# Retention attention before a sine feed-forward: bursts in four 64x64 tiles, head-wise loads of two batches, and decay and state hand-on on GpSimd

## Chip, cores and metric

One core of one Trainium2 chip. The metric is device time of one execution in microseconds (us), from several executions of each kernel. Kernels that are compared ran in the same rounds on one chip; experiments 1 to 4 ran on one chip and 5 to 12 on another, where the kernel before took 219.49 and 219.7 to 219.8 us. "The profile" is one execution recorded by the hardware profiler; "the trace" is its list of instructions. PE is TensorE, PEld its weight loads, DVE VectorE, ACT ScalarE, POOL GpSimd, SP SyncE. In the code, matmuls write tiles of PSUM; all other tiles stand in SBUF. All times and ratios of the text are of fast runs; one run of the kernel before (222.21 us, slow) is left out of the ratios.

## The reference, cut to what matters

```python
# q, k, v: 4 batches x 8 heads x 768 positions x 64, float32
for t in range(S):                                   # attention: a decaying state per head
    state = gamma[h] * state + outer(k[t], v[t])
    y[t]  = scale * (q[t] @ state)
x = y as [3072 tokens, 512]
h = x @ w_in                                         # 512 -> 2048
g = h + sin(alpha * h) ** 2 / (alpha + 1e-9)
out = g @ w_out                                      # 2048 -> 512
```

Both kernels cut the 768 positions into six chunks of 128. For a chunk after the first of its batch, the work on TensorE is a **burst**: *inter* (state times q), *scores* (k times q, then masked), *mix* (v times masked scores) and *sums* (k times v, the addition to the state). Bursts are put between the dense matmuls of the feed-forward, which runs over seven groups of chunks; group g+1's chunks are made while group g is in the feed-forward. The order is: the four first chunks (group 0), then batch 0's other five, batch 1's, batch 2's, batch 3's. Chunks are numbered in that order from 0: 4 is the first after the four first chunks, and 14 is the first of batch 2 after its first chunk, and 14 to 23 are batches 2 and 3. One group's feed-forward is a *phase*, cut into 16 *slots* (8 in the groups of two chunks), and a burst or a part of it is put into a slot. In the code cuts `P[n]` is chunk n and `e1` to `e3` are the first chunks of batches 1 to 3; the numbers before the brackets are slots, with T a transpose on TensorE, X one by DMA, A the scores, M inter and mix, SK the sums of a first state, and B a whole burst.

## The kernel before, where the change touches it

```python
def load_chunk(j, names="qkv"):            # 128 positions x 8 heads: 1024 rows a DMA
    ...
            nc.gpsimd.dma_start(out=t, in_=chunk_of(src, j))
def turn(j):                               # q, k transposed by a DMA of SyncE's queue
    nc.sync.dma_start_transpose(out=st["qkT", j], in_=raw["qk", j]...)
def stage_A(j):                            # scores: two tiles of 64 rows at a time
    ...
    nc.tensor.matmul(pa[:, e, p, :], qkT[r, NP + p, :], qkT[r, p, :], ...)
    nc.vector.tensor_mul(aT, pa, mask)
def stage_S(j):                            # sums: the state accumulates in PSUM
    nc.tensor.matmul(ps[64*e:64*e+64, p, :], raw["k", j][...], raw["v", j][...], start=(c == 0 and p == 0), ...)
def keep_S(j, ps):                         # hand-on: ScalarE casts it for the next chunk
    for e in range(2):
        nc.scalar.copy(s_bd[(j % NCH + 1) % 2][r, :, r], ps[r, :, :])
# ... (cut: transposes, stage_M with inter and mix, the Slot class of the feed-forward)
# GpSimd's order: each later chunk's three loads, with one earlier chunk's decay of v between
for n in range(11, NJ + 2):
    scale_v(P[n - 2], nc.gpsimd)
    if n < NJ:
        load_chunk(P[n])
    if n in (13, 15):
        scale_v(P[(n - 9) // 2], nc.gpsimd)
```

## Time and profile before

| | before |
|---|---|
| time, median of 3 runs | 219.66 us (219.4 to 219.67) |
| profiled span | 217.5 us |
| TensorE busy | 94 % of the span |
| decays of v on GpSimd | 21 of 1.056 us |
| q, k, v loads by GpSimd | 70 of about 0.9 us each |

The page's slices divide the span into 40 equal parts; a digit is the busy share in tenths, and PEclk is TensorE's granted clock in tenths of full speed. Before:

```profile
POOL 8975335999889885896981000000000000000000
PEclk9999999999999999999999999999999999999999
```

GpSimd is a queue of loads with decays between them, at work until slice 21 (about 117 us; with gaps in slices 3 to 6) and idle after. The lines that carry the reading of TensorE stand in the prediction below.

### The profile page before, as it was taken

What the parts mean: (1) busy time and instruction counts of PE and PEld (TensorE: products, weight loads), DVE (VectorE), ACT (ScalarE), POOL (GpSimd) and SP (SyncE); (2) the same over time, 40 slices, a digit from 0 to 9 for tenths busy, and PEclk for the clock granted to TensorE, in tenths of its full rate; (3) what the DMA queues carried; (4) which work ended last, traced back from release to release, by engine and by line L of the source; (5) the groups of instructions that cost most, each with busy time, mean ns of one, the idle gap of its engine ahead of it and who ended that gap; (6) DMA issues with size and microseconds to landing.
All of it is one profiled execution on the core that took longest, in us unless ns stands there. A gap on an engine that the chain in (4) does not pass through costs nothing.

```text
span 217.5 us, 4218 instructions
## 1 busy us (share of the span) xinstructions
PE 203.8 (94%) x1634; PEld 107.5 (49%) x1661; DVE 128.1 (59%) x213; ACT 162.8 (75%) x311; POOL 90.1 (41%) x105
## 2 busy tenths in 40 slices
PE   7798899999989999999999999999999999999992
PEld 3444554467764545445455445454544544555540
DVE  4686659867895767766466566366464555233310
ACT  7678796658889999789768768777868876766610
POOL 8975335999889885896981000000000000000000
PEclk9999999999999999999999999999999999999999
DMA  9999999999999999999999146237011101111121
GB/s 132 151 193 191 205 207 164 154 207 161 164 151 182 163 120 154 112 160 175 135 188 107 23 96 77 60 60 96 7 47 51 48 0 51 48 48 48 51 94 50
DMA packets 99508, 24.67 MB, mean 113 GB/s; under 512 B 92304, under 2 KB 96416, under 8 KB 99488
## 3 DMA queue, kind: packets, MB, share of 16 engines
q0 software_dynamic: 77024, 13.37, 84.0%
q1 hardware_dynamic: 22464, 11.02, 26.4%
q8 instruction: 13, 0.21, 0.4%
q14 instruction: 7, 0.06, 0.1%
HBM read 27.27 MB, written 6.29 MB: 154 GB/s over the span
## 4 chain that ended last, share of the span: by engine, by line
PE 74%; DVE 9%; DMA 4%; POOL 4%; ACT 4%; issue 3%; POOLq 0%; ACTq 0%
PE po L304 35%; PE ph L279 31%; DMA qkr<-in_k_dram 4%; DVE gT L294 4%; PE py L247 3%; PE pa L213 2%; POOL qkr L83 2%; ACT s L282 2%; DVE aT L217 2%; PE py L251 2%; POOL vr L83 1%; DVE xT L258 1%; PE ps L227 1%; DVE s L289 1%; ACT s L287 1%
## 5 line engine op out<-in xcount | busy, mean ns | idle before, releaser
L294 DVE SCALAR_TENSOR_TENSOR gT<-s,rec_alpha,ph 128x512 bf16<-128x512 f32 (+3 forms) x120 | 74.1, 637 | 68.1 <-ACT s L287 67.5
L279 PE MATMUL ph<-xT,w_in 128*128 128x512 bf16 (+3 forms) x478 | 97.9, 336 | 1.1 <-DVE gT L294 0.6
L304 PE MATMUL po<-w_out,gT 128*128 128x512 bf16 x360 | 94.1, 379 | 3.8 <-issue 2.9
L282 ACT ACTIVATE s<-ph,alpha_sb 128x512 f32<-128x512 f32 (+3 forms) x120 | 69.6, 601 | 34.0 <-PE ph L279 33.9
L279 PEld LDWEIGHTS <-w_in 128*128 128x128 bf16 x480 | 45.5, 98 | 42.6 <-issue 2.1
L287 ACT ACTIVATE s<-s 128x512 f32<-128x512 f32 (+1 forms) x94 | 58.4, 621 | 2.6
L304 PEld LDWEIGHTS <-gT 128*128 128x128 bf16 x384 | 35.2, 98 | 38.2 <-issue 0.6
L112 POOL TENSOR_TENSOR vr<-vr,kg 128x512 bf16<-128x512 bf16 x21 | 22.0, 1056 | 12.2 <-DMA vr<-in_v_dram 12.2
L217 DVE TENSOR_TENSOR aT<-pa,mask 128x1024 bf16<-128x1024 f32 x20 | 24.4, 1220 | 0.3 <-PE pa L213 0.3
L83 POOL DMA_DIRECT2D vr<-in_v_dram x24 | 21.7, 904 | 3.0 <-DMA w_in<-in_moe_w_in_dram 1.7
L83 POOL DMA_DIRECT2D qkr<-in_q_dram x23 | 21.3, 925 | 4.0 <-DMA w_out<-in_moe_w_out_dram 1.6
L83 POOL DMA_DIRECT2D qkr<-in_k_dram x23 | 20.4, 887 | 3.8 <-DMA w_out<-in_moe_w_out_dram 3.3
L234 ACT CAST s_bd<-ps 64x256 bf16<-64x256 f32 x40 | 14.4, 360 | 2.4 <-PE ps L227 2.1
L316 ACT COPY o_sb<-po 128x512 f32<-128x512 f32 x23 | 13.1, 576 | 3.9 <-PE po L304 3.9
L258 DVE TENSOR_TENSOR xT<-py,qg 128x512 bf16<-128x512 f32 x20 | 13.7, 684 | 2.6 <-PE py L251 2.5
L328 PE MATMUL spare<-warm 128*128 128x512 bf16 x27 | 9.3, 465 | 1.4 <-DVE warm L131 1.2
L213 PEld LDWEIGHTS <-qkT 64*128 64x128 bf16 x192 | 5.4, 94 | 9.3 <-issue 7.1
L251 PE MATMUL py<-aT,vr 128*64 128x128 bf16 x192 | 9.5, 220 | 0.4 <-DVE rec_alpha L366 0.2
L213 PE MATMUL pa<-qkT 64*128 64x128 bf16 x192 | 9.5, 219 | 0.4 <-ACT qkT L186 0.2
L247 PE MATMUL py<-qkT,s_bd 128*64 128x128 bf16 x160 | 8.3, 224 | 0.7 <-DVE xT L258 0.7
L247 PEld LDWEIGHTS <-s_bd 128*64 128x64 bf16 x160 | 5.4, 109 | 4.8 <-issue 2.0
L251 PEld LDWEIGHTS <-vr 128*64 128x64 bf16 x192 | 6.9, 110 | 1.3 <-issue 1.0
(59 smaller groups left out, 68.8 us busy)
## 6 DMA issues: line engine op xcount, KB each, us to landing
out_dram<-o_sb SPq DMA_DIRECT2D x24, 256.0 KB, 2.3
vr<-in_v_dram POOLq DMA_DIRECT2D x24, 128.0 KB, 6.2
qkr<-in_q_dram POOLq DMA_DIRECT2D x23, 128.0 KB, 5.6
qkr<-in_k_dram POOLq DMA_DIRECT2D x23, 128.0 KB, 5.8
w_in<-in_moe_w_in_dram POOLq DMA_DIRECT2D x4, 512.0 KB, 11.1
w_out<-in_moe_w_out_dram POOLq DMA_DIRECT2D x4, 512.0 KB, 14.8
q<-in_q_dram SPq DMA_DIRECT2D x1, 256.0 KB, 3.4
k<-in_k_dram SPq DMA_DIRECT2D x1, 256.0 KB, 4.7
```

Of the source, the lines that this page charges most:

```text
L83: nc.gpsimd.dma_start(out=t, in_=chunk_of(src, j))
L112: eng.tensor_mul(raw["v", j], raw["v", j], kg[:, j % NCH, :, None].to_broadcast([128, H, D]))
L213: nc.tensor.matmul(pa[:, e, p, :], qkT[r, NP + p, :], qkT[r, p, :], start=(p == 0), stop=True, skip_group_check=True)
L217: nc.vector.tensor_mul(aT.rearrange("p e n t -> p (e n) t"), pa.rearrange("p e n t -> p (e n) t"), m)
L247: nc.tensor.matmul(py[r, p, :], s_bd[c % 2][:, p, r], qkT[:, p, :], start=(p == 0), stop=True, skip_group_check=True)
L251: nc.tensor.matmul(py[64 * e:64 * e + 64, p, :], vs[:, 2 * p + e, :], aT[:, e, p, :], start=(c == 0 and p == 0), stop=True, skip_group_che ...
L258: nc.vector.tensor_mul(x, py, qg[:, c])
L279: nc.tensor.matmul(self.ph[:, m, :], w_in[:, i, f * 128:(f + 1) * 128], xT[g][:, i, self.lo:self.hi], start=(m == 0 and i == 0), stop=(i = ...
L282: nc.scalar.activation(out=self.s[:, m, :], in_=self.ph[:, m, :], func=ACTF.Sin, scale=alpha_sb[:, f:f + 1])
L287: nc.scalar.activation(out=self.s, in_=self.s, func=ACTF.Square)
L294: nc.vector.scalar_tensor_tensor(gT[self.g][:, f, self.lo:self.hi], self.s[:, m, :], rec_alpha[:, f:f + 1], self.ph[:, m, :], op0=ALU.mult ...
L304: nc.tensor.matmul(po[g, ts], gT[g][:, f, ts * C:(ts + 1) * C], w_out[:, f, :], start=(f == 0), stop=(f == FF - 1))
```

## The change

Its intent: shorter bursts (all four 64x64 tiles of TensorE at once; for batches 2 and 3 a head-wise layout that leaves out the scores above the diagonal and runs inter in the full array), VectorE's and ScalarE's burst work taken out of the way of the feed-forward's additions, and state and decay of the head-wise chunks on GpSimd, which has time late in the kernel. The diff cut to its core (cut: tables, masks, renamed tiles, the new start, the slot arithmetic):

```diff
+    def wide(j):                                   # the head-wise chunks
+        return j % NCH > 0 and j // NCH >= 2
+    def load_seq(bt):                              # a whole batch: 24 DMAs of 640 rows
+        for i, src in enumerate((q, k, v)):
+            for h in range(H):
+                nc.gpsimd.dma_start(out=o, in_=src[bt, h, C:, :].rearrange("(f i) d -> i f d", i=64))
     def load_w_in(i):                              # 1 DMA becomes 3; the last two exchange row halves
+        nc.gpsimd.dma_start(out=w_in[:, 0:2, c], in_=w_in_v[:, 0:2, c])
+        for y in range(2):
+            nc.gpsimd.dma_start(out=w_in[64 * y:64 * y + 64, 2:4, c], ...)
-    def keep_S(j, ps):                             # ScalarE, from PSUM
+    def keep(j, py, base=256):                     # VectorE adds the sums to a float state in SBUF
+            nc.vector.tensor_add(s_f, s_f, new)
+    def hand_on(j):
+        if not wide(j + 1):
+            nc.scalar.copy(s_n[i], s_f)
+            return
+        nc.gpsimd.tensor_copy(s[half(0), :, 0:4:3], s_f[half(0)])
+        nc.gpsimd.tensor_copy(s[half(1), :, 1:3], s_f[half(1)])
-    for n in range(11, NJ + 2):                    # loads and decays in turn
-        scale_v(P[n - 2], nc.gpsimd)
-        if n < NJ:
-            load_chunk(P[n])
+    load_chunk(P[11])
+    scale_v(P[9], nc.gpsimd)
+    load_chunk(P[12])
+    load_chunk(P[13])
+    load_seq(2)
+    load_seq(3)                                    # later decays and hand-ons stand behind these
-     5: [A(P[8]), M(P[7])], 6: [X(P[11]), A(P[9]), M(P[8]), SK(e1)], 7: [M(P[9])]}, 2)
+     5: [X(P[11]), B(P[8], P[9], e1)], 7: [B(P[9], P[10])]}, 2, calm=False, hold=6)
+    def burst(old, new, first=None):               # inter(old), scores(new), mix(old), sums
-    for fn in out_pieces(NG - 1, range(sizes[-1])):
+    for fn in out_pieces(NG - 1, range(sizes[-1] - 1)):
+    last_tile(NG - 1, sizes[-1] - 1)               # leaves in 256, 128 and 128 columns
```

## The prediction

> **What bounds the kernel now.** I read the page's totals first, then its chain of work that ended last, then TensorE's waits in the steady part, then the timeline of one attention burst, then GpSimd's timeline and the tail.
>
> ```profile
> PE 203.8 (94%) x1634; PEld 107.5 (49%) x1661; DVE 128.1 (59%) x213; ACT 162.8 (75%) x311; POOL 90.1 (41%) x105
> PE 74%; DVE 9%; DMA 4%; POOL 4%; ACT 4%; issue 3%; POOLq 0%; ACTq 0%
> ```
>
> TensorE is busy for 94% of the span and carries 74% of the chain. TensorE's own waits between 66 and 214 us are these, all of them:
>
> ```profile
> PE po L304 <- issue: 1.9, 12, 0.2
> PE py L247 <- DVE xT L258: 0.2, 1, 0.2
> PE ph L279 <- ACT o_sb L316: 0.2, 1, 0.2
> ```
>
> So for 148 us no other engine is in TensorE's way: only less TensorE work helps there, and every new wait costs its full length. (Waits just under the view's cut add some 0.6 us around 78 and 88 us.) One burst in that part, in TensorE's timeline with its weight loads:
>
> ```profile
> 100.26 1.03 PE L279 MATMUL ph<-xT,w_in 128*128 128x512 bf16 x4
> ...
> 101.22 0.40 PE L213 MATMUL pa<-qkT 64*128 64x128 bf16 x8
> ...
> 101.55 0.41 PE L247 MATMUL py<-qkT,s_bd 128*64 128x128 bf16 x8
> ...
> 101.79 0.39 PE L251 MATMUL py<-aT,vr 128*64 128x128 bf16 x8
> ...
> 102.02 0.29 PE L227 MATMUL ps<-vr,qkr 128*64 128x64 bf16 x8
> 102.23 0.55 PEld L304 LDWEIGHTS <-gT 128*128 128x128 bf16 x4
> 102.47 0.81 PE L304 MATMUL po<-w_out,gT 128*128 128x512 bf16 x3 [0.16 <-issue]
> ```
>
> Read the starts, not the durations: matmuls are pipelined. Dense groups of four follow each other every 0.865 us, 0.216 us for a matmul of 512 columns. The burst therefore begins at 100.26 + 0.86 = 101.12. It ends about 102.25, where po's weights are loaded: four loads stand against three matmuls, so the first matmul's record is missing. That is 1.13 us. Its parts: way in 0.10, scores 0.33 with the change of mode after them, state times q 0.24, mix 0.23, sums 0.12, way out 0.11. The next burst's scores start at 109.25: the period of 8.03 us less 32 dense matmuls at 0.216 (6.91) leaves 1.12 us, the same.
>
> **What the Trainium skill says.** (1) "TensorE: Matmul & The Clock Gate", Part 1, gives N / 2.4 GHz + about 2.5 ns from start to start when warm: 216 ns at 512 columns and 56 at 128. The trace agrees with 216 and, in the eight pairs of the mix, with 4 rounds in 0.23 us: two column tiles run side by side at 57 ns a round. (2) "TensorEngine Tiling (Array Packing)" says under Overview that 64x64 gives four independent tiles, and under Key Properties that changing the tiling mode drains the array. The trace shows about 0.1 us at each change; four tiles at once no trace here shows yet. (3) "GPSIMD Engine Reference", Engine selection, says that GpSimd has no PSUM port, which is why the new hand-on reads a float copy of the state that VectorE keeps in SBUF. (4) "DMA: Bandwidth & Descriptors", SWDGE vs HWDGE vs iDMA, says that descriptors of GpSimd's DMAs are written by GpSimd's own cores. The trace agrees: an issue of 1024 rows holds GpSimd 0.88 us.
>
> ```profile
> 42.55 0.89 POOL L83 DMA_DIRECT2D vr<-in_v_dram  x1
> 43.91 1.04 POOL L112 TENSOR_TENSOR vr<-vr,kg 128x512 bf16<-128x512 bf16 x1 [0.46 <-DMA vr<-in_v_dram]
> 44.90 0.94 POOL L83 DMA_DIRECT2D qkr<-in_q_dram  x1
> 45.84 0.88 POOL L83 DMA_DIRECT2D qkr<-in_k_dram  x1
> ```
>
> **The change, part by part.** *Bursts on TensorE.* Batches 0 and 1 (10 chunks after the first ones) get inter and scores in 64x64 tiles, with mix and sums as before: inter 2 rounds of 56 ns = 0.11, scores 4 x 0.056 = 0.22, mix 0.22, sums 4 x 0.031 = 0.12, three changes of mode 0.30. Sum 0.98 us against 1.13: saves 0.15, times 10 = 1.5 us. Batches 2 and 3 (10 chunks): inter in the full array, 4 x 0.056 = 0.22 and no change of mode before it; scores without the block above the diagonal, 2 x (0.056 + 0.031) = 0.17; mix 0.17; sums 0.12; two changes 0.20. Sum 0.89: saves 0.23, times 10 = 2.3 us. Together **3.8 us**, all on the path. A count over both built programs with these rates (four tiles side by side, 0.1 us a change) gives 201.3 us of TensorE stream before and 197.6 after: 3.7.
>
> *Vector work.* A burst's mask moves ahead of the slot's last addition, keep and exit into the next slot. Per burst VectorE loses nothing but gains a state addition (estimate 0.42 us, from the 0.68 of a 128x512 multiplication); the head-wise mask has 768 columns in place of 1024 (1.22 to about 0.94). ScalarE loses the state casts: 40 of 360 ns, 14.4 us. VectorE is at 59% and ScalarE at 75%, and TensorE does not wait for them from 66 us on, so this is worth only the waits before: TensorE's gaps from 45 to 65 us (0.3, 0.5, 0.3 us and some smaller) and the 0.6 around 78 and 88. I take **1.5 us**. Against it stand VectorE's new tables, masks and memsets in the start, a good dozen small instructions of 0.06 to 0.5 us, and the copy of the first state between 24 and 38 us, where the chain does run over gT and s: +0.5 us.
>
> *Loads.* w_in comes in 12 DMAs in place of 4. GpSimd pays about 8 x 0.7 us more, but from 20 to 36 us its issues stand 2.5 us apart and wait 1.6 each for the DMA queue, so that hides. Batches 2 and 3 come head by head in 48 DMAs of 640 rows, after batch 1 and before any decay or hand-on that stands behind them in GpSimd's order.
>
> *Tail.* The last tile goes out in pieces of 256, 128 and 128 columns.
>
> ```profile
> 209.99 0.59 ACT L316 COPY o_sb<-po 128x512 f32<-128x512 f32 x1 [2.87 <-PE po L304]
> 213.44 0.42 DVE L313 COPY o_sb<-po 128x256 f32<-128x256 f32 x1 [6.23 <-PE po L304]
> 213.90 0.37 ACT L314 COPY o_sb<-po 128x256 f32<-128x256 f32 x1 [3.33 <-DVE o_sb L313]
> ```
>
> Here two copies stand in a row, then 256 KB leave. One short copy (about 0.25 us) and 64 KB take their place: **0.8 us**. The sum: 3.7 + 1.5 + 0.8 - 0.5 = 5.5 us, or 214.2 us.
>
> **The rivals.** *A: GpSimd's queue becomes a wait.* The first chunk of batch 2 must be decayed on GpSimd before its sums, in slot 13 of the third group's phase, and that decay stands behind all 48 head loads. TensorE would be there at about 84 us (phase starts near 64, 13 slots of 1.30 us and three bursts). GpSimd: the load of chunk 7 starts at 37.8 as now; seven loads of 2.6 us and five decays of 1.05 bring it to about 62. How long is an issue of 640 rows? The trace has 0.87 for 1024 and 0.73 for 512 rows (w_in), so a straight line gives 0.77, 48 x 0.77 = 37 us, and the decay is done at 100: a stall of 15 us, 229 us in all. If the fixed part belongs to the 128 partitions rather than to the instruction, 64 partitions cost near 0.5 and the decay is done at 87: 3 us, 217. For A speaks the order of instructions and the two durations; against it, that the stall would be so plain in a profile that slots tuned this finely would hardly have kept it. I give a stall over 2 us one chance in three. *B: four tiles don't run side by side* (weight loads of 64 columns or the issue of eight instructions per round limit it): a round of 128 columns then costs 0.11 and both kinds of burst come to 1.1 us or more; the gain falls to about 2 us, 217.5. The row pairs and column pairs both overlap fully in the trace, so I give it one in eight. *C: buffers.* VectorE's mask delays the addition that frees ph; the present kernel delays it by mask and exit together and waits for nothing, so this is small.
>
> **Range and chances.** Without A and B 213 to 215.2; B lands at 216 to 218; A spreads from 216 to 229. The middle of the mixture is **214.8 us**, and 8 in 10 lie within **211.8 to 222**. Faster by over 2% means under 215.3: 0.57. Within 2%: 0.30. Slower by over 2% (over 224.1): 0.13, nearly all of it A.
>
> **What would show it.** Burst to burst in the late phases 7.8 us in place of 8.03 at the same dense matmuls; a burst of head-wise chunks 0.9 us from the last ph to the first po; scores of four tiles starting within some 15 ns of each other and then 56 ns later. VectorE and ScalarE not in TensorE's waits. Rival A shows as one wait of TensorE's sums for the decay around 84 us, with GpSimd's row of DMA issues right up to it; rival B as rounds of over 80 ns. I am wrong if the time leaves 211.8 to 222, or if the gain comes from elsewhere than bursts, early waits and tail.

## The result and the profile after

| | before | after |
|---|---|---|
| time, median of 4 fast runs of the same rounds | 219.53 us (218.95 to 219.67) | 240.86 us (240.02 to 242.13) |
| ratio of fast runs | | 1.098, 95% interval 1.092 to 1.104 |
| profiled span, mean clock | 217.5 us, 0.999 | 239.6 us, 0.964 |

Ratios here and below are the mean time of one kernel's fast runs over that of the other's of the same rounds, so not quite the ratio of the medians. The change made the kernel slower by 9.8%. The page's lines that answer to those of before:

```profile
PE 204.3 (85%) x1921; PEld 109.5 (46%) x1949; DVE 136.8 (57%) x249; ACT 152.6 (64%) x281; POOL 106.4 (44%) x147
PE   8896798788958998003999999999999999999994
POOL 8976658899644689899032043302130030000000
PEclk9999999999999999755899999999999999999999
PE 51%; DMA 29%; POOL 16%; issue 2%; DVE 0%; POOLq 0%; DVEq 0%
```

TensorE's busy time is the same, but in slices 16 and 17 (96 to 108 us) it does nothing, while GpSimd is full; the clock is at 5 to 8 tenths in slices 16 to 19. (The clock record of this trace has only full and half: half from 98.6 to 115.7 us.) The chain that ended last now runs 29% over DMA and 16% over GpSimd. TensorE's largest waits (us in total, times, longest):

```profile
PE py L311 <- POOL vr L142: 15.3, 1, 15.3
...
PE pa L363 <- DMA qkT<-qkr: 2.2, 1, 2.2
```

TensorE's timeline around the first wait (start, duration, operation; in brackets the idle time before it and its releaser):

```profile
95.68 0.41 PE L390 MATMUL py<-aT,vr 128*64 128x128 bf16 x8
111.39 0.42 PE L311 MATMUL py<-vr,qkr 128*64 128x64 bf16 x8 [15.29 <-POOL vr L142]
112.57 1.91 PE L439 MATMUL ph<-xT,w_in 128*128 128x512 bf16 x4
...
118.42 1.03 PE L439 MATMUL ph<-xT,w_in 128*128 128x512 bf16 x4
```

The sums of the first state of batch 2 wait for the decay of that chunk's v. The four matmuls after it take 1.91 us, those at 118.42 take 1.03. GpSimd's timeline over the same stretch:

```profile
65.16 0.73 POOL L104 DMA_DIRECT2D qk_seq<-in_q_dram  x1
67.29 0.72 POOL L104 DMA_DIRECT2D qk_seq<-in_q_dram  x1 [1.41 <-DMA vr<-in_v_dram]
69.59 1.42 POOL L104 DMA_DIRECT2D qk_seq<-in_q_dram  x2 [1.58 <-DMA qkr<-in_q_dram]
...
104.52 5.75 POOL L104 DMA_DIRECT2D v_seq<-in_v_dram  x8
110.16 1.17 POOL L142 TENSOR_TENSOR vr<-vr,kg 128x512 bf16<-128x512 bf16 x1
```

From 65.16 to 110.16 us GpSimd does nothing but the 48 head-wise loads: 48 issues of about 0.72 us (34.4 us) and 10.8 us of waits between them, which the trace ends with the landing of earlier loads. Then comes the decay for which TensorE has stood since 96.

**Where the 22.1 us of the profiled spans came from.** A landmark is the start of the first weight load of w_in of a group's feed-forward, read in both traces.

| landmark | before | after | after less before | added in this stretch |
|---|---|---|---|---|
| group 1 | 48.00 | 51.97 | +3.97 | +4.0 |
| group 2 | 64.59 | 71.51 | +6.92 | +3.0 |
| group 2, slot 12 | 83.45 | 91.75 | +8.30 | +1.4 |
| group 3 | 90.73 | 116.48 | +25.75 | +17.4 |
| last w_in load | 204.39 | 227.53 | +23.14 | -2.6 |
| end | 217.54 | 239.64 | +22.10 | -1.0 |

So three things happened: the first third lost 7 to 8 us, one wait cost 17, and the steady part and the tail gained 3.6. Of the 17.4, 15.3 is the wait itself and about 2 the half clock after it: in the trace dense matmuls of 512 columns start 0.43 us apart from 112.1 to about 115.6 and 0.216 after. "TensorE: Matmul & The Clock Gate" of the Trainium skill, Part 1 ("What's actually happening"), says that after an idle window of about 3.4 us TensorE falls to half its clock, and its next heading ("Wait — 56ns, not 53.3ns?") gives 426.7 ns for 512 columns at that clock. This trace agrees on the rate (0.43 us after 15 us of idle time). Its clock fell at 98.6 us, 2.5 us after TensorE's last matmul ended; in experiments 1 and 3 it fell in waits of 2.0 and 3.9 us.

The gain in the steady part is the one predicted. A head-wise burst, in TensorE's timeline:

```profile
127.12 0.39 PE L347 MATMUL py<-qkT,s_w 128*128 128x128 bf16 x4
127.44 0.25 PE L372 MATMUL pa<-qkT 64*64 64x128 bf16 x4
...
127.81 0.30 PE L314 MATMUL py<-v_seq,qk_seq 64*64 64x64 bf16 x16
128.26 0.38 PE L463 MATMUL po<-w_out,gT 128*128 128x512 bf16 x1 [0.16 <-issue]
```

The next burst ends 7.84 us later (first matmul of po at 136.10), less 32 dense matmuls at 0.216 (6.91): 0.93 us a burst, against 0.89 predicted and 1.13 before. Ten of them are worth 2.0 us; the landmarks say 2.6 for the whole stretch, and the other 0.6 is not accounted for. The four tiles of a round start 3 to 4 ns apart. The tail:

```profile
233.12 0.59 ACT L467 COPY o_sb<-po 128x512 f32<-128x512 f32 x1 [2.87 <-PE po L463]
...
236.71 0.29 DVE L484 COPY o_sb<-poh 128x128 f32<-128x128 f32 x1 [0.60 <-PE poh L478]
```

One copy of 0.29 us stands after the last matmul where before there were two in a row (0.42 and 0.37); from the last w_in load to the end is 12.11 us in place of 13.15.

### The profile page after: what moved, and what is told of

Read it like the earlier page. It is cut to its first block, busy times and chain, and to the rows that moved or that the text cites. A ratio compares the mean times of both kernels' runs of the same rounds, so it can differ in the third digit from the quotient of the medians.

```text
span 239.6 us, 4842 instructions
## 1 busy us (share of the span) xinstructions
PE 204.3 (85%) x1921; PEld 109.5 (46%) x1949; DVE 136.8 (57%) x249; ACT 152.6 (64%) x281; POOL 106.4 (44%) x147
## 4 chain that ended last, share of the span: by engine, by line
PE 51%; DMA 29%; POOL 16%; issue 2%; DVE 0%; POOLq 0%; DVEq 0%
PE po L463 25%; PE ph L439 21%; DMA qk_seq<-in_q_dram 7%; DMA w_in<-in_moe_w_in_dram 6%; DMA qkr<-in_q_dram 5%; DMA w_out<-in_moe_w_out_dram 5%; POOL qkr L89 4%; POOL v_seq L104 4%; DMA vr<-in_v_dram 3%; POOL qk_seq L104 3%; DMA qk_seq<-in_k_dram 3%; POOL vr L89 3%; POOL vr L142 3%; PE poh L478 1%; PE py L347 1%
## 5 line engine op out<-in xcount | busy, mean ns | idle before, releaser
L332 POOL CAST s_w<-s_f 64x256 bf16<-64x256 f32 x10 | 3.9, 392 | 61.8 <-DVE s_f L323 55.9
L311 PE MATMUL py<-vr,qkr 128*64 128x64 bf16 x88 | 3.4, 200 | 15.3 <-POOL vr L142 15.3
L89 POOL DMA_DIRECT2D vr<-in_v_dram x14 | 12.7, 907 | 4.7 <-DMA qkr<-in_q_dram 2.2
L104 POOL DMA_DIRECT2D qk_seq<-in_q_dram x16 | 11.5, 759 | 6.4 <-DMA qkr<-in_q_dram 3.9
L104 POOL DMA_DIRECT2D qk_seq<-in_k_dram x16 | 11.4, 729 | 4.0 <-DMA qk_seq<-in_q_dram 4.0
L89 POOL DMA_DIRECT2D qkr<-in_q_dram x13 | 11.9, 919 | 2.0 <-DMA w_out<-in_moe_w_out_dram 1.2
L89 POOL DMA_DIRECT2D qkr<-in_k_dram x13 | 11.7, 900 | 2.3 <-DMA w_out<-in_moe_w_out_dram 1.6
L367 DVE TENSOR_TENSOR aT<-pa,mask 128x1024 bf16<-128x1024 f32 x10 | 12.2, 1217 | 0.5 <-PE pa L363 0.5
L104 POOL DMA_DIRECT2D v_seq<-in_v_dram x16 | 11.5, 763 | 0.4 <-DMA qk_seq<-in_k_dram 0.4
L142 POOL TENSOR_TENSOR v_seq<-v_seq,kgq 128x512 bf16<-128x512 bf16 x10 | 10.5, 1054 | 0.7
L381 DVE TENSOR_TENSOR aT<-pa,maskq 128x768 bf16<-128x768 f32 x10 | 9.6, 957 | 1.6 <-PE pa L376 0.5
```

The source lines that it names most:

```text
L104: nc.gpsimd.dma_start(out=o, in_=src[bt, h, C:, :].rearrange("(f i) d -> i f d", i=64))
L142: eng.tensor_mul(t, t, by[:, j % NCH, :, None].to_broadcast([128, H, D]))
L367: return {"mask": lambda: nc.vector.tensor_mul(aT.rearrange("p e n t -> p (e n) t"), pa.rearrange("p e n t -> p (e n) t"), mask_bc)}
```

## The experiments

Kernels named e... start from the changed kernel, b... from the kernel before. Each ratio is against the kernel before in the same rounds.

### 1. The decay ahead of the head-wise loads

```diff
     load_chunk(P[13])
+    scale_v(e2, nc.gpsimd)        # and taken out of its later slot
     load_seq(2)
     load_seq(3)
```

> The changed kernel with one decay on GpSimd, that of batch 2's first chunk, moved ahead of the 48 head loads; nothing else. Theory Q (the order of GpSimd's queue): the 15.3 us wait of TensorE's sums for this decay goes, but the next GpSimd work behind the loads, the hand-on of that state and the first head-wise decay, still ends near 112 us, so TensorE stands again one burst later (inter or mix of the first head-wise chunk), for some 7 us; total about 232 to 234 us, a gain of 7 to 9. Rival D (the data of these chunks lands too late, whoever decays): the chunk's v landed long before, but the wait would stay at about the same place and the total at 239 to 241.

Measured: 236.29 us, ratio 1.075 (1.071 to 1.080); clock 0.964 again. TensorE's largest wait:

```profile
PE py L347 <- POOL s_w L333: 9.2, 1, 9.2
```

The wait for the decay is gone, and TensorE stands one step later for the next thing that GpSimd has to do, the hand-on of the state. It is GpSimd's queue and not that one decay. The gain of 4.6 us was smaller than the 7 to 9 expected: the stall was 9.2 rather than 7 us, and there was half clock twice. The page's clock line:

```profile
PEclk9997699999999999995599999999999999999999
```

The second dip (10.2 us from 106.3) belongs to the stall. The first (6.8 us from 20.9) falls in a wait of only 2.0 us, for the loaded k of a first chunk, and the profiled run reaches group 1 2.8 us later than the changed kernel, whose program is the same up to there.

### 2. Batch 3's head-wise loads later

```diff
     load_seq(2)
-    load_seq(3)
...
+    for i in range(3):                                    # q, k, v of batch 3
+        at(FF + 4 * i, lambda i=i: load_seq(3, (i,)))     # in slots of the phase of group 3
```

> The changed kernel with batch 3's 24 head loads issued in three parts during the next group's phase, behind that phase's hand-ons, in place of before all decays. Theory Q: the decay of batch 2's first chunk runs right behind batch 2's loads, at about 92 us, before TensorE wants it at 96; the 15 us wait and the half clock after it go; about 222 to 224 us, a gain of 17 to 18. What is left above the kernel before, 3 to 4 us, would be the waits ahead of 95 us. Rival D: v of batch 2 lands only near 95 to 98 us, so a wait of 2 to 5 us at the mix of its first chunk comes in its place and the total is 225 to 228.

Measured: 224.46 us, ratio 1.024 (1.020 to 1.028), half a us above the range. The stall and the half clock are gone (clock 1.000; the decay ends at 92.0 us): same instructions, half of the head-wise loads behind the decay and hand-on instead of ahead. With this, 16.4 of the 21.3 us between the two medians are shown to be the order of GpSimd's queue. What is left is lost ahead of group 3: this kernel is 6.9 us later than the kernel before at group 2's landmark, 8.5 at group 3's and 4.8 at the end. Its largest wait:

```profile
PE pa L368 <- DMA qkT<-qkr: 4.3, 3, 2.3
```

The transposed q and k of chunks come late from the DMA. In the kernel before there was no such wait.

### 3. Batch 2 loaded chunk by chunk again

```diff
     def wide(j):
-        return j % NCH > 0 and j // NCH >= 2
+        return j % NCH > 0 and j // NCH >= 3
...
-    load_seq(2)
+    load_chunk(P[14])
+    scale_v(e2, nc.gpsimd)
+    for i in range(15, 19):
+        load_chunk(P[i])
+        scale_v(P[i - 1], nc.gpsimd)
+    scale_v(P[18], nc.gpsimd)
+    scale_v(e3, nc.gpsimd)
     load_seq(3)
```

> The changed kernel with batch 2 loaded and worked chunk by chunk as batches 0 and 1, its decays on GpSimd between the loads; only batch 3 head by head. Theory Q: no wait for GpSimd; the first chunk of batch 2 is there long before; bursts of batch 2 cost 7.9 us a period in place of 7.84. About 221 to 223 us. If the waits ahead of 95 us come from the bursts' need of the next chunk's transposed q and k one burst earlier, and not from head-wise loads, they stay (some 6 us behind the kernel before at the start of the third group).

Measured: 225.82 us, ratio 1.028 (1.024 to 1.033). No wait for GpSimd is left, but the expectation was missed by about 3 us, with one wait:

```profile
PE pa L363 <- DMA qkT<-qkr: 3.9, 1, 3.9
```

It is chunk 9's transposed q and k, at 62 to 66 us (the "tenth chunk" of the expectations below, counted from 1). In the changed kernel the wait of this kind was for chunk 10, 2.2 us at 67 to 69. The wait cost more than its length, as half clock followed for 6.8 us from 64.5:

```profile
PEclk9999999999976999999999999999999999999999
```

All four runs have a mean clock of 0.984 to 0.992. The scores now stand one burst earlier than before, so they need these data sooner; why they come late is the question of experiments 5 to 7.

### 4. The split of w_in alone, in the kernel before

```diff
-        nc.gpsimd.dma_start(out=w_in[:, :, i * fw:(i + 1) * fw], in_=w_in_v[:, :, i * fw:(i + 1) * fw])
+        nc.gpsimd.dma_start(out=w_in[:, 0:2, c], in_=w_in_v[:, 0:2, c])
+        for y in range(2):
+            nc.gpsimd.dma_start(out=w_in[64 * y:64 * y + 64, 2:4, c], in_=w_in_v[64 * y:64 * y + 64, 2:4, c])
```

> The kernel before with w_in loaded in 12 DMAs of the changed kernel's shapes (no halves exchanged, so the result stays right). If the split makes the changed kernel's first 2 us of delay (its fourth chunk's k lands at 20.6 us in place of 19.5), this kernel is 1 to 2 us slower than before (220.5 to 221.5) and shows the later landing; if the order of slots and tiles does it, it is within 0.3 us of before.

Measured: 219.49 us, ratio 1.001 (0.997 to 1.005). Twelve DMAs in place of four cost nothing that can be seen, as predicted. The late start is not from them.

### 5. Loads one step further ahead of the decays

```diff
 (from experiment 3)
     load_chunk(P[8])
-    scale_v(P[6], nc.gpsimd)
     load_chunk(P[9])
-    scale_v(P[7], nc.gpsimd)
+    scale_v(P[6], nc.gpsimd)
     load_chunk(P[10])
+    scale_v(P[7], nc.gpsimd)
+    load_chunk(P[11])
     ...
```

> The kernel with only batch 3 head by head (225.8 us), with each decay on GpSimd moved one load further back, so that the loads of chunks 9 to 13 are issued 1 to 3 us earlier. Theory I (the order of issue on GpSimd sets when the tenth chunk's q and k land): the 3.9 us wait of TensorE's scores for their transposed form shrinks by 2 to 3 us; 223 us. Theory T (the DMA engines themselves are the limit in that stretch, as the transposes through DMA take a share of them): the loads are issued earlier and land when they did; the wait stays within 1 us; 225 to 226 us.

Measured: 226.60 us, ratio 1.031 (1.025 to 1.037). The waits for transposed q and k are 4.7 us in place of 3.9, shared by more chunks (1.4 for chunk 9, 2.5 for chunk 10, 0.6 for chunk 11). Chunk 10's k was issued 2.2 us earlier than in experiment 3 (48.6 us) and landed no earlier (60.6 against 60.3); chunk 9's landed 2.9 us earlier (53.4), but that is where the changed kernel has it with the old order (53.2). So the order of issue is not what makes these loads late. The profiled run was the fastest of the four and the only one with a clock above 0.99; the others were not traced.

### 6. Two chunks transposed on TensorE

```diff
 (from experiment 3; before, chunks 6 and 7 were transposed on TensorE, 8 by DMA)
-    turn(P[6])
+    stage_T(P[6], nc.scalar)
...
-    turn(P[8])
...
-    2: [X(P[10])],
+    2: [T(P[8]), X(P[10])],
```

> The same kernel (225.8 us) with chunks 6 and 8 transposed on TensorE in place of by DMA (the kernel before has chunk 6 on TensorE, the changed one by DMA). TensorE pays 0.9 us for the two, and a copy of 0.7 to 1.0 us each on ScalarE and VectorE. Theory T: two DMA transposes fewer between 44 and 55 us, loads of chunks 9 and 10 land 2 to 4 us earlier, the wait for the tenth chunk goes from 3.9 to about 1 or less; 223 us or a little under. Theory I: landing unchanged, the wait stays, 226 to 227 us.

Measured: 222.05 us, ratio 1.012 (1.005 to 1.018), 3.8 us less than experiment 3 (on the other chip; experiments 5 and 7, on this one, took 226.6 and 226.4). Its wait at the same line:

```profile
PE pa L363 <- DMA qkT<-qkr: 0.8, 1, 0.8
```

It is for chunk 12, at 79 to 80 us; those for chunks 9 and 10 are gone, and with them the half clock (1.000 in all four runs). This speaks for the shared DMA engines: GpSimd issued chunk 10's k at 50.4 us, as in experiment 3 (50.8), and it landed at 55.3 in place of 60.3, chunk 9's at 52.8 in place of 56.3. From 45 to 55 us GpSimd's DMA queue moved 8803 packets, against 5470 in experiment 3 and 6656 in the changed kernel. The changed kernel transposes chunk 6 by DMA where the kernel before did it on TensorE, and does chunk 8 earlier, just where loads of q, k and v are still what everything waits for. How much of the 3.8 us is wait (3.1) and how much clock was not separated.

### 7. Two mends of the first group's end

```diff
 (from experiment 3)
-    F((0, 1), (15,))
+    both last matmuls of the first two output tiles, then both copies
...
-    run(burst(P[4], P[5]), "keep", "hand", "mask", "exit")
+    run(burst(P[4], P[5]), "keep", "hand", "exit", "mask")
```

> The same kernel (225.8 us) with two orders mended in the stretch around 43 to 50 us: both last matmuls of the first two output tiles ahead of the copies out of them (the two tiles are halves of one PSUM tile, so the second's matmul waits for the copy of the first, 1.3 us in the trace), and the exit of chunk 4 ahead of the mask of chunk 5 (0.5 to 0.7 us wait for the single py). If the waits are what they look like, the start of the second group comes 1.5 to 1.9 us earlier; but if the tenth chunk's q and k bind right after, the wait there grows by as much and the total stays at 225 to 226; otherwise 224.

Measured: 226.43 us, ratio 1.031 (1.026 to 1.036): no gain over experiment 3. TensorE reaches group 1 only 0.3 us earlier, where 1.5 to 1.9 was expected: of the 1.6 us of waits that the two mends took away, 0.7 came back as a wait for the moved copies, and the profiled run was 0.6 us later at chunk 4's scores, ahead of both mends. Chunk 9's wait ends at 65.5 us (66.0 in experiment 3) and is about as long (3.7), with 3.4 us of half clock after it. As long as the loads set the time, what TensorE saves ahead of them is handed back there.

### 8. The last tile in pieces, in the kernel before

```diff
-    for fn in out_pieces(NG - 1, range(sizes[-1])):
+    for fn in out_pieces(NG - 1, range(sizes[-1] - 1)):
         fn()
+    last_tile(NG - 1, sizes[-1] - 1)
```

> The kernel before with the changed kernel's last output tile in pieces of 256, 128 and 128 columns, nothing else. From the traces the stretch from the last load of w_in to the end is 13.15 us before and 12.1 after: 0.8 to 1.1 us faster than before, 218.5 us.

Measured: 218.82 us, ratio 0.996 (0.990 to 1.002). By time this is unclear. In the trace the tail is 12.16 us in place of 13.15, as in the changed kernel, so the mechanism is there, though its 1 us is not told from noise by the clock: the first landmark of this run was 1.5 us later than in the kernel before, which runs the same start.

### 9. All mends together

```diff
 (experiment 6 and experiment 7, and)
-    run(mix(P[5]), "exit", "keep", "hand")
+    run({**scores(P[6]), **mix(P[5])}, "exit", "keep", "hand", "mask")
 (and the copy of chunk 8's transpose on ScalarE)
```

> The kernel with only batch 3 head by head and chunks 6 and 8 transposed on TensorE (222.05 us), with the two orders of the stretch at 43 to 50 us mended, the copy of chunk 8's transposed form on ScalarE, and chunk 6's scores moved into the burst of chunk 5. These waits were 1.9, 0.3, 1.3 and 0.75 us in its trace; now that the DMA does not bind there they should no longer be handed on: 218 to 219.5 us, about level with the kernel before, with the late phases 2.6 us faster than before and the start still slower. If DMA binds again because TensorE arrives earlier, waits for transposed q and k come back and it is 220 to 221.

Measured: 221.49 us, ratio 1.008 (1.000 to 1.016): 2.0 us above the first range. What happened is the second branch of the expectation, and its range was missed by 0.5. TensorE arrived earlier, at 68.71 in place of 70.11 at group 2, and the waits for transposed q and k came back (2.0 us in place of 0.8, for chunks 12 and 14), so that at group 3 only 0.1 us was left of the 1.4. VectorE's wait (2.0) stayed as it was in experiment 6, and a wait for ScalarE's copies stayed in part (1.1 in place of 1.7).

### 10. Chunk 10 on TensorE as well

```diff
-    2: [lambda: stage_T(P[8], nc.scalar), X(P[10])],
+    2: [lambda: stage_T(P[8], nc.scalar)],
...
+    6: [lambda: stage_T(P[10], nc.scalar)],
```

> The same with chunk 10 transposed on TensorE too. 0.45 us more TensorE work; one DMA transpose fewer near 60 us. If waits for transposed q and k came back in the run beside it, this takes 1 to 2 us of them away; if not, it is 0.3 to 0.5 us slower.

Measured: 222.54 us, ratio 1.013 (1.009 to 1.018). No gain: the DMA wait fell to 0.5, and this took its place (2.0 in experiment 9). (The edit moved chunk 10, for which experiment 9 did not wait.)

```profile
PE ph L439 <- DVE gT L454: 3.5, 5, 1.5
```

### 11. No head-wise chunk at all

```diff
 (from experiment 9)
-        return j % NCH > 0 and j // NCH >= 3
+        return j % NCH > 0 and j // NCH >= 4          # none; all chunks loaded and decayed in turn
```

> The first of these with no head-wise chunk at all: batch 3 is loaded and worked chunk by chunk too. Head-wise bursts save 0.08 us each on TensorE by the count (0.90 against 0.98), five of them 0.4 us; so 0.3 to 0.5 us slower than the first, within noise. More than that would mean that head-wise chunks also help in another way, less that the gain of the late phases comes from the four tiles and not from the head-wise form.

Measured: 222.02 us, ratio 1.013 (1.007 to 1.019), within noise of experiment 9. Two chunk-wise bursts that follow each other:

```profile
130.16 0.31 PE L352 MATMUL py<-qkT,s_n 64*64 64x128 bf16 x8
...
138.10 0.31 PE L352 MATMUL py<-qkT,s_n 64*64 64x128 bf16 x8
```

The period is 7.94 us, less 6.91: 1.03 us a burst, against 0.98 predicted, 0.93 for the head-wise form and 1.13 before. So the four tiles alone give 0.10 a burst, and the head-wise form with its loads another 0.10, at most 0.5 us for the five chunks left in experiment 9.

### 12. The order of before with the new bursts

```diff
 (from experiment 11: the kernel before's order of loads, decays, first slots and late
  scores up to the end of batch 1, with four-tile bursts, the new hand-on and the new tail)
-    run(burst(P[4], P[5]), "keep", "hand", "exit", "mask")
+    run(scores(P[5]))
...
+    at(1, A(P[10]))
```

> The four-tile bursts, the vector work's new places and the last tile in pieces, but no head-wise chunk, and up to the end of batch 1 the order, the loads, the transposes on TensorE and the scores' late places of the kernel before; bursts one ahead only from batch 2 on. If the loss of the changed kernel is one of feeding (GpSimd's queue, DMA engines, scores one burst ahead) and the tiles are what they were counted to be, the start of the fourth group comes at 89 to 91 us as before, the phases to the last group take 92 us in place of 94.6 and the tail 12.1 in place of 13.15: 214.5 to 216.5 us, 1.5 to 2.3% faster than before. If the four-tile form itself costs in the early phases, it stays at 218 to 220.

Measured: 222.98 us, ratio 1.016 (1.012 to 1.021): missed by over 6 us. The transposed q and k are no longer waited for, but now inter has to wait. The trace around one such wait:

```profile
63.51 0.41 DVE L323 TENSOR_TENSOR s_f<-s_f,py 128x256 f32<-128x256 f32 x1
...
63.99 0.39 ACT L329 CAST s_n<-s_f 128x256 bf16<-128x256 f32 x1
64.83 0.84 ACT L442 ACTIVATE s<-ph,alpha_sb 128x256 f32<-128x256 f32 x2 [0.46 <-PE ph L439]
64.98 0.68 DVE L403 TENSOR_TENSOR xT<-py,qg 128x512 bf16<-128x512 f32 x1
...
65.81 0.31 PE L352 MATMUL py<-qkT,s_n 64*64 64x128 bf16 x8 [1.01 <-ACT s L442]
```

The hand-on is now a VectorE addition (0.41 us) and then a ScalarE cast (0.39); before it was the casts alone, from a state that accumulated in PSUM. But this wait is not for the state: its cast ended at 64.38, and the list names the sine only because it ended last. Inter writes py, of which there is one buffer, and VectorE's multiplication out of the py of the chunk before ended at 65.66, just ahead of inter; it had stood behind the addition and the mask (1.22). So it is with the other wait of 1.0, at 69.2 us; one of 0.9, at 95.3, is put down to that multiplication, and only one of 0.6, at 50.9, to the cast. What has grown is VectorE's queue between two bursts in neighbouring slots. That the order of before does not suit the new hand-on is thus argued from these waits; no run moved the addition alone. (The profiled run, one of the two longest of the six at 224.55 us, also lost clock at the start: half for 3.4 us from 25.9.)

No kernel tried here beats the kernel before by more than noise. The nearest is experiment 8.

## Why the prediction was wrong, point by point

- **Bursts, 3.8 us on the path.** Mechanism right, sizes nearly: 0.93 us head-wise (0.89 predicted) and 1.03 chunk-wise (0.98). The ten head-wise ones gave 2.0 us of the 2.3. The other ten, of batches 0 and 1, gave nothing at the end: they lie ahead of 91 us, where the changed kernel is later at every landmark.
- **Rival B**, tiles not side by side, is refuted: tiles start 3 to 4 ns apart.
- **Tail, 0.8 us.** Right: 1.04 in the trace.
- **w_in's split** hides: right (experiment 4).
- **Vector work, 1.5 us gained, 0.5 lost.** Wrong in sign. Up to group 2's landmark VectorE is busy 53.0 us where it was 48.2, and TensorE's listed waits there are 11.7 us against 6.4, which is 5.3 of the 6.9 us lost by then. The step took the early waits as what the change removes, and did not ask which waits the earlier scores and the moved transposes would make. 2.2 us of them is the DMA wait for chunk 10, which experiment 6 takes away; the rest is spread over waits for VectorE and ScalarE of about 1 us or less. Experiments 9 and 10 show that mending one brings another. How much of the rest belongs to each added VectorE instruction, and how much to scatter in when the first loads land (1.5 us between runs with the same start), stays open.
- **Rival A**, GpSimd's queue. This is what happened, and **the failed step is the weight it was given**: the main sum has no term for it. The straight line between two measured durations gave 0.77 us an issue and a stall of 15 us; a guess that half as many partitions would cost less, and the argument that slots tuned so finely would hardly have kept so plain a stall, brought the chance to one in three. Measured: 0.72 us an issue, a stall of 15.3 us. That the length agrees so well is partly luck. The line's first point, 0.73 us for 512 rows of w_in, is a misreading (the trace has 0.75 to 0.83). And both ends came 11 to 12 us later than worked out (TensorE at 96 in place of 84, the decay at 111 in place of 100). What the working left out on GpSimd's side is 10.8 us of waits for the DMA queue between the issues, and a queue that begins 3 us later; on TensorE's side 8 of the 12 us, lost up to slot 12 of group 2. The half clock after the stall, some 2 us, was not in it either. Experiments 1 and 2 show the cause: move the one decay, and a later GpSimd instruction, the hand-on, stalls TensorE; move half of the loads, and the stall is gone.
- **Rival C**, buffers, is small in the changed kernel, as expected: matmuls into ph waited 0.9 us for the addition that frees it, against 0.6 before. In experiments 6, 9 and 10 it grew to 2.0, 2.0 and 3.5 us; once, at 59.6 us of experiment 6, 1.2 us behind a mask (1.22) and a multiplication on VectorE.

Put together: +4.0, +3.0 and +1.4 us in the first third and the start of group 2, +17.4 for the stall and its clock, -2.6 for the bursts, -1.0 for the tail make the 22.1 us of the profiled spans.

## What to carry to other kernels

An engine that issues DMAs and also computes is a queue in program order: before moving work onto it, add up the issues that stand ahead of that work, with measured durations and with the waits for the DMA queue that the trace shows, and compare with the time at which the work is needed. If that sum says that there is a stall, believe the sum. And a share saved on the bound engine counts only where that engine is the bound: in the first third of this kernel, where loads and vector work set the pace, every mend on TensorE came back as another wait. A wait can also cost more than its length: in three traces here half clock came with waits of 2.0 to 3.9 us.

## What the Trainium skill lacked or had wrong

- "DMA: Bandwidth & Descriptors", Anatomy of one DMA, calls descriptor generation "small, variable" and puts the fixed cost on completion. Here generation held GpSimd for 0.72 us for a 640-row DMA and about 0.9 us for a 1024-row one, all through the issuing engine's own work: 48 of them and their queue waits kept a decay of 1.17 us back for 45 us. The page has no figure for issue time by rows.
- The same page, DMA Transpose (X-bar), says nothing of what a transpose takes from loads that run beside it. Here, with two chunks' transposes moved to TensorE, GpSimd's queue moved 8803 packets in place of 5470 from 45 to 55 us, a load issued at the same time landed 5.0 us sooner, and the kernel gained 3.8 us.
- "TensorEngine Tiling (Array Packing)", Key Properties, says that changing the tiling mode drains TensorE and gives no figure. In these traces a change costs 0.09 to 0.11 us; three of them are over a quarter of a burst of 1.03 us.
- "TensorE: Matmul & The Clock Gate", Part 1, agreed with the runs on the rate: 0.43 us from start to start after 15 us of idle time, for about 4 us. Its table puts the fall to half clock after at least one idle window of about 3.4 us. Here less was enough: the clock fell 1.7 us into a wait of 2.0 us (experiment 1) and 2.4 us into one of 3.9 (experiment 3), and it did not fall in waits of 2.2 to 2.5 us (changed kernel, experiments 2 and 5).
